# Key logits of the second batch in an agent attention followed by a two-layer network: whole-row products into one bank

## The chip, the core and the metric

The kernel runs on one core of a Trainium2 chip. The metric is the device time of one execution in microseconds (us). The core has a matrix engine (TensorE, PE in the profile, with its weight loads listed apart as PEld), a vector engine (VectorE, DVE), a scalar engine (ScalarE, ACT), GpSimd (POOL) and a queue engine (SP) that issues DMAs. TensorE multiplies a stationary operand, which it loads first, with a moving operand, and writes into PSUM, which has eight banks. VectorE and ScalarE read PSUM.

## The reference

Two batches of 12480 queries, keys and values of 128 channels, and 49 agents per batch. The agents attend to the keys, the queries attend to the agents, and the result goes through a two-layer network with a PReLU between its layers:

```python
a2k = sm(agents, k)          # softmax over the keys of scale * agents @ k.T
agent_v = a2k @ v            # 49 x 128 per batch
q2a = sm(q, agents)          # softmax over the agents
x = (q2a @ agent_v).reshape(24960, 128)
h = x @ w_in                 # 128 -> 2048
g = maximum(h, 0) + alpha * minimum(h, 0)
out = g @ w_out              # 2048 -> 128
```

Softmax subtracts the maximum and adds 1e-9 to the sum. Everything is float32 outside.

## The kernel before

A prologue of some 62 us treats the first batch's keys and values and prepares the weights. Then comes one main loop of 416 steps: 52 groups of 480 queries, 8 steps (`NM`) for a group, two of the 16 blocks of 128 hidden channels a step. A step has two parts, which the loop at the end of the kernel writes out by hand. `g1(s + 2)` (line 968) multiplies the folded first layer with the softmax weights of the queries, three products for each of two halves, into a PSUM tile `h`; ScalarE takes relu of it into `rh` (line 974), and VectorE the remainder into `rl` (line 975). `g2(s)` (line 990) multiplies `rh` and `rl` with the second layer, six products for each half, into a PSUM tile `acc`. All of these are half-array products: `TILES` names the rows 0 to 63 and 64 to 127, and each product runs over one half of the rows into a bank of its own, so that the two halves can run side by side. At the last step of each group, line 1001 adds three further half products, two on one half and one on the other; which half gets two alternates with the group.

Everything else is put between the steps by a table, `plan`, which says at which step which function is called: the queries' softmax for later groups (`q_...`), the outputs of earlier groups, and from step 16 on the second batch's keys, from step 96 on its values, and from 189 on the folding of its weights. There is no scheduler: each engine's order is the order in which the code issues.

The second batch's keys come in units of 512, which VectorE transposes into `kt` (line 538). `k_logits` is called for two units at a time, at steps 6, 9 and 14 of every 16 from step 16 on (`KEYS`), between the step's `g1` and its `g2`: twelve calls with two units of four blocks of 128 keys, and a thirteenth, at step 86, with the last unit, two blocks of 96 keys. For each block the keys are the stationary operand and the 49 agents the moving one. The products are plain float32, whereas the main loop's are in the one-pass form of float32. `pair_tile` gives a tile of two banks; the first half of the channels is multiplied into the first bank and the second half into the second. One step later, ahead of that step's `g1`, `k_take` has ScalarE copy the first bank's logits into `s` (line 572), and VectorE add the second bank's to them (line 574). `k_max_keys` on VectorE then takes a maximum of `s`.

Of the kernel before, what the change touches and what calls it, by code (L numbers as in the profile page):

```python
# [13 lines left out]
ALU = mybir.AluOpType  # L14
# [41 lines left out]
def kernel(  # L56
# [11 lines left out]
    nc = tc.nc  # L68
    B, N, C = q.shape
    NA = agents.shape[1]  # L70
# [9 lines left out]
    UB = KT // P  # L80
# [25 lines left out]
    TILES = ((0, HALF), (HALF, P))  # L106
# [3 lines left out]
    def pair_tile(name, i=None):  # L110

        i = (step[0] // NM + 1) % 2 if i is None else i
        return late[i].tile([P, 2, 512], F32, tag="x", name=name)


    def blocks(u):

        n = min(KT, N - u * KT)
        nb = -(-n // P)
        assert n % nb == 0  # L120
        return u * KT, n // nb, nb


    def wide(p):
# [25 lines left out]
    st = [  # L150
        dict(rows=2 * NA, cols=2 * C + 2) if b else {} for b in range(B)
    ]
# [215 lines left out]
    kv = {}  # L368
# [170 lines left out]
        kv["kt", b, u] = kt  # L539

    def k_logits(b, us):
        t = pair_tile(f"kl{b}_{us[0]}")
        tiles = [(t[:, i, :], r0, r1) for i, (r0, r1) in enumerate(TILES)]
        got = kv["kl", b, us[0]] = []
        c0 = 0
        for u in us:
            _, rows, nb = blocks(u)
            kt = kv.pop(("kt", b, u))
            for n in range(nb):
                c = c0 + n * NA  # L550
                for d, r0, r1 in tiles:
                    nc.tensor.matmul(  # L552
                        d[0:rows, c : c + NA], lhsT=kt[r0:r1, n * rows : (n + 1) * rows],
                        rhs=st[b]["ag"][r0:r1, 0:NA], start=True, stop=True,
                    )
            if got and got[-1][1] == rows:
                got[-1][2] += nb
            else:
                got.append([u, rows, nb, c0, [d for d, _, _ in tiles]])
            c0 += nb * NA  # L560

    def scores(b, u):
# [1 line left out]
        return st[b]["s"][0:rows, u * UB : u * UB + nb, :]  # L564

    def k_take(b, us):
        for u, rows, nb, c0, ds in kv.pop(("kl", b, us[0])):
            to = st[b]["s"][0:rows, u * UB : u * UB + nb, :]
            lg = [
                d[0:rows, c0 : c0 + nb * NA].rearrange("p (n a) -> p n a", a=NA) for d in ds  # L570
            ]
            nc.scalar.copy(out=to, in_=lg[0])
            for x in lg[1:]:
                nc.vector.tensor_tensor(out=to, in0=x, in1=to, op=ALU.add)

    def k_max(b):

# [469 lines left out]
    with tc.manual_schedule():  # L1047
# [18 lines left out]
        for p in range(NPK):  # L1066
            at(4 * p, k_turn, p)
            a, b = divmod(p, 2)
# [25 lines left out]
        for n in range(7):  # L1094
            load, ops = (load_win, narrow_win) if n < 4 else (load_wo, narrow_wo)
            s = SLABS[n]
# [11 lines left out]
        def more():  # L1108
            f = next(loads, None)
            if f is not None:  # L1110
                f[1](*f[2:])
            return f

        while n_in < N_IN:
            f = more()
            n_in += f[1] not in (q_load_rows, load_alpha, load_late)
        for s in range(max(plan) + 1):
            for f, a in plan.pop(s, ()):
                f(*a)
                if f.__name__ == "total" or f in (k_turn, k_mix):  # L1120
                    while True:
                        f = more()
# [40 lines left out]
        for g in range(NGT):  # L1163
            s0 = g * NM
            at((g + 1) * NM + OUT[0], o_take, g)
            d = OUT[1 if g % 2 == 0 or g == NGT - 1 else 2]
# [14 lines left out]
        for c, (lo, hi) in enumerate(pieces):  # L1181
            s0 = KEYS_FROM + c // len(KEYS) * 16
            turn, log, top = KEYS[c % len(KEYS)]
            us = tuple(range(lo, hi))
            for u, s in zip(us, turn):
                load(load_kb, "k", u, s0 + s)
                at(s0 + s, k_transpose_dve, 1, u)
            at(s0 + log, k_logits, 1, us)
            pre(s0 + log + 1, k_take, 1, us)
            if hi != NU - 1:  # L1190
                at(s0 + top, k_max_keys, 1, min(c, len(parts) - 1))
            last = s0 + top
        at(last + 1, k_max, 1)
        assert last + 3 < VALUES_FROM
        for c, (lo, hi) in enumerate(parts):
            s0 = VALUES_FROM + c // len(VALUES) * 16
            steps, av = VALUES[c % len(VALUES)]
            us = list(range(lo, hi))
# [57 lines left out]
```

## Time and profile before

| | |
|---|---|
| time, median of 3 runs | 987.12 us (987.0 to 988.08) |
| span of the profiled execution, first to last instruction | 985.9 us |
| the median lies above that span by | 1.2 us |
| TensorE, products | 971.7 us busy, 99% of the span |
| TensorE, weight loads | 927.0 us, 94% |
| VectorE | 837.7 us, 85% |
| ScalarE | 626.4 us, 64% |

The profile is of one execution. Its span runs from the first instruction to the last; the time of a run also has what lies around that. Loads and products of TensorE overlap, and products overlap each other, so their busy times do not add up to a length of work: what counts is the distance from one start to the next. A product in plain float32 leaves two records, each with a load of its own.

### The profile page before, as it was taken

Reading aid. Unit: us, or ns where it says so; the run is one execution under the profiler, and the core shown is the slowest. Engines: PE = TensorE matmul, PEld = TensorE weight load, DVE = VectorE, ACT = ScalarE, POOL = GpSimd, SP = SyncE. Lnnn points to the kernel's source line nnn. Section 1 sums busy time; section 2 is a strip of 40 time slices with the busy share of each in tenths; the row PEclk is TensorE's granted clock in tenths of the full one; section 3 lists DMA queues with packets and bytes.
Section 4 is the critical chain, followed back from the end, with each engine's and each line's share of the span. In section 5 each row is a group of like instructions: output and inputs, shape, how many; then the busy total and the mean of one; then the engine's idle time right before and its main releaser. Section 6 shows DMA issues by size and latency. Waiting matters only on the chain.

```text
span 985.9 us, 21716 instructions
## 1 busy us (share of the span) xinstructions
PE 971.7 (99%) x9046; PEld 927.0 (94%) x9046; DVE 837.7 (85%) x1054; ACT 626.4 (64%) x779; POOL 89.8 (9%) x67
## 2 busy tenths in 40 slices
PE   8989999999999999999999999999999999999997
PEld 5658999999989999999987999999999999999997
DVE  7887988998899999999987788788878887888775
ACT  5765655655667767777765666666666666666563
POOL 0011011011011011001101101100110111011100
PEclk9999999999999999999999999999999999999999
DMA  9933354444234234234312222212221223121201
GB/s 342 361 51 63 65 84 87 81 70 88 42 75 80 62 73 95 45 70 95 65 31 44 42 51 41 53 37 46 52 53 31 42 55 56 35 41 33 42 11 31
DMA packets 281027, 69.51 MB, mean 71 GB/s; under 512 B 259119, under 2 KB 273953, under 8 KB 280929
## 3 DMA queue, kind: packets, MB, share of 16 engines
q1 hardware_dynamic: 279937, 68.00, 33.0%
q8 instruction: 71, 1.16, 0.5%
q10 hardware_dynamic: 992, 0.12, 0.1%
q14 instruction: 27, 0.22, 0.1%
HBM read 42.59 MB, written 12.78 MB: 56 GB/s over the span
## 4 chain that ended last, share of the span: by engine, by line
PE 94%; DVE 2%; DMA 2%; ACT 1%; issue 0%; SPq 0%; ACTq 0%
PE acc L990 55%; PE h L968 27%; PE lg L864 2%; PE kl L552 2%; PE acc L1001 2%; PE av L650 1%; PE qsum L923 1%; DMA kw<-in_k_dram 1%; DMA win<-in_moe_w_in_dram 1%; PE a_ps L726 0%; DVE red L414 0%; PE avw L471 0%; PE ktp L388 0%; PE lin_ps L784 0%; PE etp L451 0%
## 5 line engine op out<-in xcount | busy, mean ns | idle before, releaser
L975 DVE SCALAR_TENSOR_TENSOR rl<-h,rh 128x960 fp32r<-128x960 f32 x416 | 478.2, 1150 | 123.1 <-ACT rh L974 120.8
L974 ACT ACTIVATE rh<-h 128x960 fp32r<-128x960 f32 x416 | 404.3, 972 | 270.1 <-PE h L968 262.1
L968 PE MATMUL h<-qmh,sab 64*128 64x480 f32 x1664 | 401.3, 378 | 0.7 <-DVE rl L975 0.5
L990 PE MATMUL acc<-rh,wl 64*128 64x480 f32 x1664 | 400.3, 378 | 0.0
L990 PE MATMUL acc<-rh,wh 64*128 64x480 f32 x1664 | 398.0, 375 | 0.0
L990 PE MATMUL acc<-rl,wh 64*128 64x480 f32 x1664 | 313.2, 377 | 0.0
L968 PEld LDWEIGHTS h<-qmh,sab 64*128 64x128 f32 x1664 | 247.2, 185 | 7.5 <-DVE rl L975 2.5
L990 PEld LDWEIGHTS acc<-rh,wl 64*128 64x128 f32 x1664 | 246.9, 184 | 5.9 <-issue 2.3
L990 PEld LDWEIGHTS acc<-rh,wh 64*128 64x128 f32 x1664 | 247.6, 184 | 2.9
L990 PEld LDWEIGHTS acc<-rl,wh 64*128 64x128 f32 x1664 | 223.6, 184 | 3.2
L968 PE MATMUL h<-qml,sab 64*128 64x480 f32 x832 | 222.7, 377 | 0.0
L894 POOL PARTITION_ALL_REDUCE qm<-qs x26 | 85.6, 3293 | 768.0 <-DVE qs L890 731.3
L968 PEld LDWEIGHTS h<-qml,sab 64*128 64x128 f32 x832 | 128.0, 185 | 1.7 <-DVE qml L912 0.2
L1006 ACT COPY os<-acc 128x480 f32<-128x480 f32 x52 | 29.2, 561 | 33.8 <-PE acc L1001 33.6
L1007 DVE TENSOR_TENSOR os<-acc,os 128x480 f32<-128x480 f32 x52 | 33.9, 651 | 2.7 <-ACT os L1006 2.4
L1012 DVE STREAM_TRANSPOSE ot<-os 128x480 f32<-128x480 f32 x52 | 34.7, 668 | 0.0
L903 ACT ACTIVATE qmh<-qs,padb 128x960 fp32r<-128x960 f32 x26 | 28.5, 1097 | 9.2 <-DVE qs L899 9.2
L1017 DVE TENSOR_TENSOR ot<-ot,qr 128x480 f32<-128x480 f32 x52 | 33.6, 645 | 0.1
L899 DVE TENSOR_TENSOR qs<-qs,qm 128x960 f32<-128x960 f32 x26 | 29.8, 1148 | 0.5 <-POOL qm L894 0.5
L890 DVE TENSOR_TENSOR qs<-qs,qw 128x960 f32<-128x960 f32 x25 | 28.7, 1148 | 1.7 <-DMA qw<-qs 1.7
L912 DVE TENSOR_TENSOR qml<-qs,qmh 128x960 fp32r<-128x960 f32 x26 | 29.8, 1148 | 0.0
L827 DVE STREAM_TRANSPOSE qt<-qin 128x960 f32<-128x960 f32 x25 | 29.2, 1167 | 0.0
(172 smaller groups left out, 802.8 us busy)
## 6 DMA issues: line engine op xcount, KB each, us to landing
out_dram<-ot SPq DMA_DIRECT2D x206, 60.0 KB
qin<-in_q_dram SPq DMA_DIRECT2D x200, 60.0 KB
qw<-qs SPq DMA_DIRECT2D x50, 240.0 KB
kw<-in_k_dram SPq DMA_DIRECT2D x12, 512.0 KB
vw<-in_v_dram SPq DMA_DIRECT2D x12, 512.0 KB
kb<-in_k_dram SPq DMA_DIRECT2D x96, 64.0 KB
v<-in_v_dram SPq DMA_DIRECT2D x24, 256.0 KB
win<-in_moe_w_in_dram SPq DMA_DIRECT2D x4, 512.0 KB
```

Source lines behind the costliest of these rows:

```text
L827: nc.vector.transpose(out=flat(t), in_=gq.pop(("in", k)).rearrange("p h t i -> p (h t i)"))
L894: nc.gpsimd.partition_all_reduce(flat(t), flat(gq["s", k]), P, ReduceOp.max)
L899: nc.vector.tensor_tensor(out=t, in0=t, in1=gq.pop(("m", k)), op=ALU.subtract)
L912: nc.vector.tensor_tensor(out=m, in0=gq["e", k], in1=gq["mh", k], op=ALU.subtract)
L968: nc.tensor.matmul(h[:, u, 0:GT], lhsT=w[a][r0:r1, f0 : f0 + P], rhs=x[r0:r1, :], start=n == 0, stop=n == 2,)
L974: nc.scalar.activation(out=rh, in_=h[:, :, 0:GT], func=AF.Relu)
L975: nc.vector.scalar_tensor_tensor(out=rl, in0=h[:, :, 0:GT], scalar=0.0, in1=rh, op0=ALU.max, op1=ALU.subtract)
L990: nc.tensor.matmul(acc[:, i, 0:GT], lhsT=a[r0:r1, 2 * m + u, :], rhs=x[r0:r1, u, :], start=m == 0 and n == 0, stop=False,)
L1006: nc.scalar.copy(out=t, in_=acc[:, 0, 0:GT])
L1007: nc.vector.tensor_tensor(out=t, in0=acc[:, 1, 0:GT], in1=t, op=ALU.add)
L1012: nc.vector.transpose(out=t.rearrange("p t i -> p (t i)"), in_=oo.pop(g))
L1017: nc.vector.tensor_tensor(out=t, in0=t, in1=gq.pop(("r", g)).to_broadcast([P, TB, 32]), op=ALU.mult)
```

## The change

`k_logits` multiplies each block of keys in one product over all 128 channels into the first bank of the pair tile, in place of two half products into two banks. `k_take` has ScalarE copy the finished logits; VectorE's additions are gone. The steps at which the functions are called are the same.

```diff
     def k_logits(b, us):
-        t = pair_tile(f"kl{b}_{us[0]}")
-        tiles = [(t[:, i, :], r0, r1) for i, (r0, r1) in enumerate(TILES)]
-        got = kv["kl", b, us[0]] = []
+        t = pair_tile(f"kl{b}_{us[0]}")[:, 0, :]
+        got = []
+        kv["kl", b, us[0]] = t, got
...
             for n in range(nb):
                 c = c0 + n * NA
-                for d, r0, r1 in tiles:
-                    nc.tensor.matmul(
-                        d[0:rows, c : c + NA], lhsT=kt[r0:r1, n * rows : (n + 1) * rows],
-                        rhs=st[b]["ag"][r0:r1, 0:NA], start=True, stop=True,
-                    )
+                nc.tensor.matmul(
+                    t[0:rows, c : c + NA], lhsT=kt[:, n * rows : (n + 1) * rows],
+                    rhs=st[b]["ag"][:, 0:NA], start=True, stop=True,
+                )
...
     def k_take(b, us):
-        for u, rows, nb, c0, ds in kv.pop(("kl", b, us[0])):
-            to = st[b]["s"][0:rows, u * UB : u * UB + nb, :]
-            lg = [
-                d[0:rows, c0 : c0 + nb * NA].rearrange("p (n a) -> p n a", a=NA) for d in ds
-            ]
-            nc.scalar.copy(out=to, in_=lg[0])
-            for x in lg[1:]:
-                nc.vector.tensor_tensor(out=to, in0=x, in1=to, op=ALU.add)
+        t, got = kv.pop(("kl", b, us[0]))
+        for u, rows, nb, c0 in got:
+            nc.scalar.copy(
+                out=st[b]["s"][0:rows, u * UB : u * UB + nb, :],
+                in_=t[0:rows, c0 : c0 + nb * NA].rearrange("p (n a) -> p n a", a=NA),
+            )
```

On TensorE, around the first call (step 22), the order before is this; `kl` is the logits' tile, `h` and `acc` those of `g1` and `g2`:

```order
L968 MATMUL h_1629<-qmh_1242,sab_858 128x480 x2
L552 MATMUL kl_0_1646<-ag_159,kt_0_1483 128x49 x8
L552 MATMUL kl_0_1646<-ag_159,kt_1_1457 128x49 x8
L990 MATMUL acc_1459<-rh_1576,wl 128x480 x2
L990 MATMUL acc_1459<-rh_1576,wh 128x480 x2
```

And now, with the line numbers of the changed kernel:

```order
L965 MATMUL h_1629<-qmh_1242,sab_858 128x480 x2
L551 MATMUL kl_0_1646<-ag_159,kt_0_1483 128x49 x4
L551 MATMUL kl_0_1646<-ag_159,kt_1_1457 128x49 x4
L987 MATMUL acc_1459<-rh_1576,wl 128x480 x2
L987 MATMUL acc_1459<-rh_1576,wh 128x480 x2
```

The place is the same; 16 half products have become 8 whole ones. On VectorE the order around the same call was:

```order
L538 STREAM_TRANSPOSE kt_2_1615<-kb_1024_1396 128x512
L975 SCALAR_TENSOR_TENSOR rl_1637<-h_1629,rh_1636 128x960
L574 TENSOR_TENSOR s_1214<-kl_0_1646,s_1214 128x392
L975 SCALAR_TENSOR_TENSOR rl_1690<-h_1682,rh_1689 128x960
L591 TENSOR_REDUCE mx_1215<-s_1214 128x49
```

and is now:

```order
L538 STREAM_TRANSPOSE kt_2_1615<-kb_1024_1396 128x512
L972 SCALAR_TENSOR_TENSOR rl_1637<-h_1629,rh_1636 128x960
L972 SCALAR_TENSOR_TENSOR rl_1681<-h_1673,rh_1680 128x960
L588 TENSOR_REDUCE mx_1215<-s_1214 128x49
L1004 TENSOR_TENSOR os_1709<-acc_1459,os_1709 128x480
```

The addition is gone, and nothing else has moved. ScalarE's, GpSimd's and the queue engine's orders are the same in both kernels.

## Rows read from the trace of the kernel before

**Rows 1.** The page: busy time of each engine (share, instructions), and the chain.

```profile
PE 971.7 (99%) x9046; PEld 927.0 (94%) x9046; DVE 837.7 (85%) x1054; ACT 626.4 (64%) x779; POOL 89.8 (9%) x67
...
PE 94%; DVE 2%; DMA 2%; ACT 1%; issue 0%; SPq 0%; ACTq 0%
```

**Rows 2.** Windows: stretch, its us, busy PE, PEld, DVE, ACT, POOL (instructions), clock, DMA.

```profile
117.00:277.00 160.00, 160.00 (x1666) 159.07 (x1664) 141.06 (x171) 94.17 (x109) 13.26 (x4) 1.00 0.43 76
```

**Rows 3.** Waits, 117 to 282 us: who waited for whom, total, times, longest.

```profile
DVE rl L975 <- ACT rh L974: 17.4, 33, 1.7
```

**Rows 4.** Tile kl: instructions, durations in ns (min/median/max), first and last start, forms.

```profile
L552 PEld LDWEIGHTS kl<-ag,kt x392: 158/188/189, 120.6 to 275.6; 64*128 64x128 f32 x192, 64*96 64x96 f32 x4
L552 PE MATMUL kl<-ag,kt x392: 201/272/273, 120.8 to 275.6; 64*128 64x49 f32 x192, 64*96 64x49 f32 x4
L572 ACT COPY s<-kl x13: 228/487/488, 122.8 to 276.5; 128x392 f32<-128x392 f32 x12, 96x98 f32<-96x98 f32 x1
L574 DVE TENSOR_TENSOR s<-kl,s x13: 247/546/567, 124.5 to 278.5; 128x392 f32<-128x392 f32 x12, 96x98 f32<-96x98 f32 x1
```

**Rows 5.** Timeline of PE, first burst: start us, us, what, form, count.

```profile
120.60 0.43 PE L968 MATMUL h<-qmh,sab 64*128 64x480 f32 x2
...
122.52 0.51 PE L990 MATMUL acc<-rh,wl 64*128 64x480 f32 x2
122.82 0.42 PE L990 MATMUL acc<-rh,wh 64*128 64x480 f32 x2
```

**Rows 6.** Timeline of PE around the last, short burst.

```profile
274.99 0.39 PE L968 MATMUL h<-qml,sab 64*128 64x480 f32 x2
275.21 0.39 PE L968 MATMUL h<-qmh,sab 64*128 64x480 f32 x2
...
276.01 0.38 PE L990 MATMUL acc<-rh,wh 64*128 64x480 f32 x2
```

**Rows 7.** Timeline of PE around line 784, 16 whole-array products.

```profile
75.27 0.37 PE L968 MATMUL h<-qmh,sab 64*128 64x480 f32 x2
...
79.67 0.38 PE L990 MATMUL acc<-rh,wh 64*128 64x480 f32 x2
```

**Rows 8.** Timeline of PE around line 738, one whole-array product.

```profile
85.76 0.38 PE L968 MATMUL h<-qml,sab 64*128 64x480 f32 x2
85.98 0.39 PE L968 MATMUL h<-qmh,sab 64*128 64x480 f32 x2
...
87.04 0.38 PE L990 MATMUL acc<-rh,wh 64*128 64x480 f32 x2
```

**Rows 9.** Timeline of PE around line 677, one product of 98 rows, two columns.

```profile
502.51 0.39 PE L968 MATMUL h<-qmh,sab 64*128 64x480 f32 x2
502.83 0.33 PE L677 MATMUL den<-x,pair 98*98 98x2 f32 x2
...
503.42 0.38 PE L990 MATMUL acc<-rh,wh 64*128 64x480 f32 x2
```

**Rows 10.** Timeline of the weight loads, line 509: two loads for a one-column product.

```profile
60.53 0.30 PEld L509 LDWEIGHTS den_ps<-den_sum,both 128*128 128x128 f32 x2 [0.17 <-issue]
```

**Rows 11.** Timeline of PE around line 702, two products, four records.

```profile
515.82 0.58 PE L968 MATMUL h<-qmh,sab 64*128 64x480 f32 x2
...
517.30 0.38 PE L990 MATMUL acc<-rh,wh 64*128 64x480 f32 x2
```

**Rows 12.** Timeline of PE around the three half products of line 1001.

```profile
507.78 0.38 PE L990 MATMUL acc<-rh,wh 64*128 64x480 f32 x2
...
508.65 0.38 PE L1001 MATMUL acc<-qml,zh 64*128 64x480 f32 x1
508.65 0.58 PE L968 MATMUL h<-qmh,sab 64*128 64x480 f32 x2
```

**Rows 13.** Lines 784 and 726: durations of products of 128 and of 512 columns, ns.

```profile
L784 PE MATMUL lin_ps<-wo,lin x32: 275/275/377, 75.6 to 79.1; 128*128 128x128 f32 x32
L726 PE MATMUL a_ps<-win,avt x16: 592/592/697, 61.9 to 535.3; 128*128 128x512 f32 x16
```

More of the change, by code (lines that the diff above doesn't have):

```diff
@@ L558, in k_logits @@
             else:
-                got.append([u, rows, nb, c0, [d for d, _, _ in tiles]])
+                got.append([u, rows, nb, c0])
             c0 += nb * NA
```

## The prediction

> **What bounds the kernel now.** I read the page first, for the engine that is never idle: TensorE's multiplications are busy for 971.7 of 985.9 us, and the chain that ended last is TensorE for 94% of its length [rows 1]. Then the stretch that the change touches: the 13 key-logit bursts (`k_logits`) run from 120.8 to 275.6 us [rows 4], and in 117 to 277 us TensorE is busy for 160.00 of 160.00 us, VectorE for 141.06 and ScalarE for 94.17 [rows 2]. In that stretch VectorE waits for ScalarE's `rh` for 17.4 us [rows 3], and no row of the waits has TensorE waiting for either. So here a microsecond more or less on TensorE is one on the end, and VectorE's work is covered as long as it is less than TensorE's. A busy TensorE need not be a fast one, so the third reading is the pitch: how long after one pair of half products the next one starts. It is 0.22 us in the main loop inside the stretch [rows 6] and outside it [rows 8], so nothing in the stretch is drawn out.
>
> **How a burst is priced.** I take the start of the last main-loop pair before a burst (line 968) and the start of the second main-loop pair behind it (line 990); the first behind it is skipped because its record contains its wait. Without a burst that distance would be two pitches, 0.44 us, in every case, so differences between cases need no further correction. A full burst takes 122.82 - 120.60 = 2.22 us [rows 5], thus 1.78 us of its own for 32 load-and-multiply records (each of its 16 half products in float32 leaves two). The two halves run side by side, so that is 16 turns of 0.111 us. The short last burst (96 keys instead of 128, two blocks) takes 276.01 - 275.21 = 0.80 us [rows 6].
>
> **Removed: half of TensorE's records.** 392 records become 196, all over 128 rows; the products have the same 49 columns. What paces a turn? Two whole-array loads of 128 columns, for products of a single column, take 0.30 us together where one load takes 0.188 [rows 10, 4]: they start 0.11 us apart, though there is next to nothing to multiply. So a load over 128 rows takes as long as two loads side by side over 64, and 16 turns stay 16 turns of about 0.11 us. I credit nothing for the halving.
>
> **Added: two changes of shape per burst.** The burst now stands, with the whole array, between half-array products. Four places of the trace of before do just that, in the main loop. The 16 float32 products of line 784 (32 records) take 79.67 - 75.27 = 4.40 us [rows 7]; the one product of line 738 (2 records) takes 87.04 - 85.98 = 1.06 us [rows 8]. The 30 records between them cost (4.40 - 1.06) / 30 = 0.111 us each, the same turn as in the bursts of today. What stays beside turns and the two pitches is 1.06 - 0.44 - 2 x 0.111 = 0.40 us: loads are no longer fetched ahead of the last products, and the other way round behind it. Today's bursts have nothing of this: 1.78 us is all turns. The last product's own length is in the 0.40: a product of 512 columns is 592 - 275 = 317 ns longer than one of 128 [rows 13], 0.83 ns a column, so 49 columns instead of 128 end 0.065 us sooner. A burst of 16 turns should thus take 1.06 + 14 x 0.111 - 0.065 = 2.55 us, which is +0.33. The other estimate starts at the narrowest such place, line 677, with loads of 98 columns and products of 2: 503.42 - 502.51 = 0.91 us for 2 records [rows 9]. By the 0.11 us of a load of 128 columns, one of 98 takes 0.083, 0.025 less; so 0.91 + 2 x 0.025 + 14 x 0.111 + 47 x 0.00083 = 2.55 us again. For the short burst: 0.91 + 2 further loads of 96 columns at 0.083 + 0.04 = 1.12 us against 0.80, +0.32. Together 12 x 0.33 + 0.32 = 4.3 us. I take that; bounds are 0.30 a burst, which is what line 677 leaves beside turns and pitches (0.91 - 0.44 - 2 x 0.083) with next to no product, and 0.40, if no product ends sooner: 3.9 to 5.2 us.
>
> **Added: the halves are brought into step.** At the end of each group of 8 steps line 1001 gives three half products to two halves. Starting in step, pairs then last 0.58 us instead of 0.38: one half lags by 0.20 [rows 12]. Today the next group's three products go the other way and close the gap again; the bursts in half rows leave it as it is. A whole-array burst must wait for the later half, and the earlier one loses its lead. Line 702 shows it: it begins with pairs of 0.58 us and takes 517.30 - 515.82 = 1.48 us for 4 records [rows 11], where 1.06 + 2 x 0.111 = 1.28 would be due: 0.20 more, measured from the half that leads. Averaged over the halves it is 0.10, and the average counts, because the three products would have cost the second half less the next time. The bursts stand at steps 6, 9 and 14 of 16, the three products at the ends of steps 7 and 15. So the bursts at 9 (four) and at 6 (five, of which the first starts at a lag of 0.05, pairs of 0.43 us in [rows 5]) lose 0.10, those at 14 nothing: 8 x 0.10 + 0.02 = 0.8 us. Bounds: nothing, if the main loop makes it up, and 1.0.
>
> **Removed: VectorE's additions.** Twelve of 0.546 us and one of 0.247 [rows 4], 6.8 us. They are covered wholly by TensorE today [rows 2, 3], so I count nothing for the end. ScalarE's copies stay, at their places. `k_max_keys` on VectorE now waits for the copy; the addition ahead of it waited for the same copy, so nothing new is held up behind it, and the `rl` of the step between them now goes first. The second bank is no longer used and the first is released earlier; no TensorE row waits for such a release, so that is zero too. If the cover were gone (a TensorE that is faster than VectorE there), the additions would be worth up to 6.8 us; with TensorE slower, as I expect, it grows.
>
> **The sum.** +4.3 + 0.8 = +5.1 us. All of it falls where TensorE is never idle, so nothing behind it absorbs it: later stretches shift as a whole. The profiled execution's span becomes 985.9 + 5.1 = 991.0 us. The median before, 987.12, lies 1.2 above that span, which does not change: 992.2 us.
>
> **Rivals.** *Loads pass one at a time (faster).* If the 32 records of today were a single row of loads, each 1.78 / 32 = 0.056 us, half as many would take 0.89 us. With the change of shape (0.335) that is 1.23 against 1.78, -0.56 a full burst, +0.14 for the short one, +0.8 for the lag: -5.7 us, 981.4. It decides from the point where a whole-array load takes under 0.09 us. The halving of the loads speaks for it; against it are the two loads 0.11 us apart [rows 10] and line 784's turns of 0.111. In the Trainium skill, page "TensorE: Matmul & The Clock Gate", Part 2, a load's time goes by its columns and not by its rows, which would make this rival's first half true; it does not say that loads of two halves queue, and the rows here have them side by side. Chance 0.04.
>
> *The change of shape is free here (same).* The waits at lines 784, 738, 677 and 702 could come from something else there, an operand that arrives late. Then 16 turns replace 16 turns, no lag is lost: 987.1. For it: the profile puts no name to most of these waits. Against: four places with different operands have the same cost within 0.05 us. Chance 0.04.
>
> *Loads and products take turns (much slower).* Side by side, a load may run under the other half's product; a whole-array load may have to wait until the product of the same rows is through. A turn is then 0.11 + 49 x 0.00083 = 0.15 us, a full burst 16 x 0.15 + 0.335 = 2.74 against 1.78, +0.95, the short one +0.5: 12 x 0.95 + 0.5 + 0.8 = +12.7 us, 999.8. Against it: line 784 has turns of 0.111 with loads of 0.11 and products of 128 columns that alone last 0.11, so there they do overlap [rows 7, 10, 13]. The Trainium skill, same page, Part 3 ("The mechanism"), says that a load overlaps running products only when their rows of the array differ, which is this rival; Part 2 of the page also allows it into a background buffer, which is what line 784 shows. Chance 0.06.
>
> **How the numbers follow.** The forecast, two shape changes a burst and the lag, has 0.86: 992.2 us. Its bounds are 3.9 and 6.2 us (5.2 + 1.0) above 987.12, 991.0 to 993.3; the runs before spread over 1.1 us, so I add 0.6 at the low and 0.5 at the high end: 990.4 to 993.8. The rivals lie outside and hold 0.14. What a measurement of this kernel can tell from no change is about 0.2%, 2 us: faster 0.04, same 0.04, slower 0.92.
>
> **What would show it.** In the profile after: 196 records at the logits' line over 128 rows, starting 0.11 us apart (0.056 for the first rival, 0.15 for the third); 2.5 to 2.6 us from the last pair before a full burst to the second behind it; pairs of 0.38 us behind each burst, and 0.58 ahead of those at steps 6 and 9; an idle stretch of the loads of about 0.3 us ahead of each burst; VectorE some 7 us less busy with no effect on the end. The forecast is wrong if the burst takes 2.2 us, or if the burst takes 2.55 and the span does not grow by it, because TensorE then had slack that I did not see.

## The result and the profile after

The changed kernel takes 993.26 us (median of 4 runs, 992.23 to 993.58) where the kernel before takes 987.60 (4 runs). The ratio is 1.0054 with a 95% interval of 1.0039 to 1.0068: slower by 3.9 to 6.7 us, where 5.1 were forecast. The profiled span is 991.8 us instead of 985.9.

The page of the changed kernel, busy times and chain (to be held against [rows 1]):

```profile
PE 979.2 (99%) x8850; PEld 912.9 (92%) x8850; DVE 832.4 (84%) x1041; ACT 626.5 (63%) x779; POOL 89.8 (9%) x67
...
PE 94%; DVE 4%; ACT 1%; issue 1%; ACTq 0%
```

TensorE has 196 records fewer (98 whole products stand in place of 196 half ones, two records each) and is busy for longer; the weight loads and VectorE are busy for less. The same stretch as in [rows 2], in the same columns, and the instructions of the logits' tile (the counterpart of [rows 4]), with what they waited for:

```profile
117.00:277.00 160.00, 160.00 (x1425) 141.32 (x1423) 132.27 (x155) 90.76 (x105) 13.26 (x4) 1.00 0.43 74
```

```profile
L551 PEld LDWEIGHTS kl<-ag,kt x196: 159/192/193, 121.7 to 281.3; 128*128 128x128 f32 x192, 128*96 128x96 f32 x4
L551 PE MATMUL kl<-ag,kt x196: 248/275/312, 121.7 to 281.3; 128*128 128x49 f32 x192, 128*96 128x49 f32 x4
L568 ACT COPY s<-kl x13: 232/487/488, 123.7 to 282.0; 128x392 f32<-128x392 f32 x12, 96x98 f32<-96x98 f32 x1
...
  issue: 4.4, 13
```

TensorE is as full as before, and in the same 160 us it gets through 1425 records instead of 1666. The halving of the logits' records accounts for most of the difference; the rest is work of the loop that now falls later. The additions' row is gone. A new one has come: the loads sat idle ahead of each of the 13 bursts, 4.4 us in all, 0.34 each. The timeline of the loads shows it at the first burst:

```profile
121.13 0.23 PEld L965 LDWEIGHTS h<-qmh,sab 64*128 64x128 f32 x2
121.69 1.86 PEld L551 LDWEIGHTS kl<-ag,kt 128*128 128x128 f32 x16 [0.34 <-issue]
123.61 0.19 PEld L987 LDWEIGHTS acc<-rh,wl 64*128 64x128 f32 x2
```

The products in the timeline of PE, first burst (step 22, see [rows 5]), second (step 25) and third (step 30):

```profile
121.35 0.42 PE L965 MATMUL h<-qmh,sab 64*128 64x480 f32 x2
121.69 1.99 PE L551 MATMUL kl<-ag,kt 128*128 128x49 f32 x16
123.61 0.48 PE L987 MATMUL acc<-rh,wl 64*128 64x480 f32 x2
123.93 0.38 PE L987 MATMUL acc<-rh,wh 64*128 64x480 f32 x2
...
127.19 0.37 PE L998 MATMUL acc<-qml,zh 64*128 64x480 f32 x1
127.20 0.59 PE L965 MATMUL h<-qmh,sab 64*128 64x480 f32 x2
...
129.59 0.59 PE L965 MATMUL h<-qmh,sab 64*128 64x480 f32 x2
130.11 1.99 PE L551 MATMUL kl<-ag,kt 128*128 128x49 f32 x16
...
132.35 0.37 PE L987 MATMUL acc<-rh,wh 64*128 64x480 f32 x2
...
141.69 0.38 PE L965 MATMUL h<-qmh,sab 64*128 64x480 f32 x2
142.01 1.99 PE L551 MATMUL kl<-ag,kt 128*128 128x49 f32 x16
...
144.25 0.38 PE L987 MATMUL acc<-rh,wh 64*128 64x480 f32 x2
```

From the last pair ahead to the second pair behind, the bursts take 2.58, 2.76 and 2.56 us, against 2.22 before. The later full bursts are alike: 2.59 to 2.62 us at step 6 of 16, 2.75 or 2.76 at step 9, 2.55 or 2.56 at step 14, and before the change 2.22 or 2.23 at every place. Behind line 998 (line 1001 before) the pairs last 0.59 us: the halves are 0.21 apart, and stay so until the second burst, behind which they last 0.37. The third burst starts with pairs of 0.38, and costs 0.20 less than the second.

The 0.34 us for which the loads sit idle is not itself the price. The first burst's products in the timeline of PE before the change, between the rows of [rows 5]:

```profile
120.81 1.93 PE L552 MATMUL kl<-ag,kt 64*128 64x49 f32 x32
```

They start 0.21 us behind the last pair (120.60); now it is 0.34 (121.69 after 121.35). So of the 0.36 us that the first burst takes longer, some 0.13 lie at its entry. With turns of the old length, the other 0.23 lie at its exit; this share is an estimate from the same rows.

The short last burst:

```profile
280.55 0.58 PE L965 MATMUL h<-qmh,sab 64*128 64x480 f32 x2
...
281.85 0.38 PE L987 MATMUL acc<-rh,wh 64*128 64x480 f32 x2
```

It takes 1.30 us, 0.20 of which is lag, against 0.80 in [rows 6].

How much of the 5.9 us of span lies in the changed stretch? Two marks that both kernels have are the products of the queries' sums (`qsum`) ahead of the first burst and behind the last. Before, then after, in the timelines of PE:

```profile
116.45 0.44 PE L923 MATMUL qsum<-qml,ones 64*128 64x480 f32 x2
...
305.15 0.38 PE L923 MATMUL qsum<-qml,ones 64*128 64x480 f32 x1
```

```profile
117.20 0.42 PE L920 MATMUL qsum<-qml,ones 64*128 64x480 f32 x2
...
311.03 0.38 PE L920 MATMUL qsum<-qml,ones 64*128 64x480 f32 x1
```

Between the marks are 188.70 us before and 193.83 after: +5.13 us. From the second mark to the end it is 680.8 us in both. The remaining 0.7 us lies ahead of the change: line 738's product, which no edit precedes, starts at 86.29 before and at 87.00 after, and in two of the kernels below, which have the same code up to there, at 85.01 and 87.04. So that part is a difference from run to run, and the distance between the marks is the better measure. I use it for the kernels below, one profiled execution of each; those for which no difference was expected agree to within 0.07 us.

| kernel | mark ahead | mark behind | between, us | to before |
|---|---|---|---|---|
| before | 116.45 | 305.15 | 188.70 | |
| after | 117.20 | 311.03 | 193.83 | +5.13 |
| half products, no addition | 116.94 | 305.64 | 188.70 | 0.00 |
| whole products, vector pass kept | 115.20 | 309.04 | 193.84 | +5.14 |
| whole products, two banks | 117.22 | 311.01 | 193.79 | +5.09 |
| products of one half only | 116.75 | 305.50 | 188.75 | +0.05 |
| half products, bursts cut | 116.69 | 305.46 | 188.77 | +0.07 |
| whole products, bursts cut | 116.11 | 313.83 | 197.72 | +9.02 |
| half products, fourth product | 116.95 | 306.63 | 189.68 | +0.98 |
| whole products, fourth product | 115.61 | 309.81 | 194.20 | +5.50 |

### The profile page after: what moved, and what is told of

Read it like the earlier page. It is cut to its first block, busy times and chain, and to the rows that moved or that the text cites. A ratio compares the mean times of both kernels' runs of the same rounds, so it can differ in the third digit from the quotient of the medians.

```text
span 991.8 us, 21311 instructions
## 1 busy us (share of the span) xinstructions
PE 979.2 (99%) x8850; PEld 912.9 (92%) x8850; DVE 832.4 (84%) x1041; ACT 626.5 (63%) x779; POOL 89.8 (9%) x67
## 4 chain that ended last, share of the span: by engine, by line
PE 94%; DVE 4%; ACT 1%; issue 1%; ACTq 0%
PE acc L987 55%; PE h L965 27%; PE kl L551 2%; PE lg L861 2%; PE acc L998 2%; PE av L647 1%; PE qsum L920 1%; DVE red L414 1%; PE a_ps L723 0%; PE ktp L388 0%; PE warm L203 0%; PE lin_ps L781 0%; DVE win L316 0%; ACT ktw L391 0%; PE avw L471 0%
## 5 line engine op out<-in xcount | busy, mean ns | idle before, releaser
L987 PEld LDWEIGHTS acc<-rh,wl 64*128 64x128 f32 x1664 | 242.4, 184 | 10.0 <-issue 2.3
L987 PEld LDWEIGHTS acc<-rh,wh 64*128 64x128 f32 x1664 | 242.9, 184 | 5.7
L987 PEld LDWEIGHTS acc<-rl,wh 64*128 64x128 f32 x1664 | 219.4, 184 | 7.0
```

The lines of the kernel that those rows point to most:

```text
L987: nc.tensor.matmul(acc[:, i, 0:GT], lhsT=a[r0:r1, 2 * m + u, :], rhs=x[r0:r1, u, :], start=m == 0 and n == 0, stop=False,)
```

## The experiments

**The additions alone.** The kernel before without line 574, so that the second half's logits are left out of the sum.

```diff
             nc.scalar.copy(out=to, in_=lg[0])
-            for x in lg[1:]:
-                nc.vector.tensor_tensor(out=to, in0=x, in1=to, op=ALU.add)
```

> The kernel before without the 13 additions on VectorE; the second half's logits are still multiplied but left out of the sum. My theory (VectorE's additions are wholly covered by TensorE): no difference to the kernel before, within 0.3 us in the span between the first and the last burst, a ratio of 1.000. Rival (VectorE holds TensorE back in this stretch): up to 6.8 us faster, the additions' own time.

Ratio 0.9999 (0.9990 to 1.0009), 0.00 us between the marks. VectorE's 6.8 us were covered entirely.

**The vector pass put back.** The changed kernel with a VectorE pass in the addition's place.

```diff
-            nc.scalar.copy(
-                out=st[b]["s"][0:rows, u * UB : u * UB + nb, :],
-                in_=t[0:rows, c0 : c0 + nb * NA].rearrange("p (n a) -> p n a", a=NA),
-            )
+            to = st[b]["s"][0:rows, u * UB : u * UB + nb, :]
+            lg = t[0:rows, c0 : c0 + nb * NA].rearrange("p (n a) -> p n a", a=NA)
+            nc.scalar.copy(out=to, in_=lg)
+            nc.vector.tensor_tensor(out=to, in0=lg, in1=to, op=ALU.max)
```

> The changed kernel with a VectorE pass of the same size put back where the addition stood (a maximum of the logits with themselves). My theory: the same time as the changed kernel, 5 to 6 us over the kernel before; a burst still takes 2.55 us from the last pair ahead of it to the second behind it. Rival (the missing addition is worth something and the change of shape costs more than read): more than 0.3 us slower than the changed kernel.

Ratio 1.0047 (1.0032 to 1.0062), 193.84 us between the marks, as in the changed kernel. The groups by line show that the pass was there:

```profile
L571 DVE TENSOR_TENSOR s<-kl,s 128x392 f32<-128x392 f32 (+1 forms) x13 | 6.8, 521 | 0.0
```

So 6.8 us of VectorE change nothing with either shape.

**Half of the products, no change of shape.** The kernel before with the products of the rows 0 to 63 alone, without additions.

```diff
-        tiles = [(t[:, i, :], r0, r1) for i, (r0, r1) in enumerate(TILES)]
+        tiles = [(t[:, i, :], r0, r1) for i, (r0, r1) in enumerate(TILES)][0:1]
...
-            for x in lg[1:]:
-                nc.vector.tensor_tensor(out=to, in0=x, in1=to, op=ALU.add)
```

> The kernel before with the second half's products and the additions left out: 16 records a burst instead of 32, all on the rows 0 to 63, no change of shape; the logits lack the second half of the channels. My theory (loads of the two halves pass side by side, a turn is one load of 0.11 us): a burst still holds up the loop by its 16 turns less what the other half runs ahead, at most one pitch of 0.22: 1.55 to 1.78 us of its own, at most 3 us faster in all. Rival (loads pass one at a time, 0.056 us each): 16 x 0.056 = 0.89 us a burst, 12 x 0.89 + 0.2 = 11 us faster than the kernel before.

Ratio 1.0001 (0.9992 to 1.0010), +0.05 us between the marks: no gain at all, where the rival had 11 us. The tile's instructions:

```profile
L552 PEld LDWEIGHTS kl<-ag,kt x196: 158/188/190, 121.0 to 275.9; 64*128 64x128 f32 x192, 64*96 64x96 f32 x4
```

With 196 loads instead of 392 the bursts hold the loop up for as long as before. The second half's loads had passed beside the first's.

**The banks.** The changed kernel with each unit's logits in a bank of its own.

```diff
-        t = pair_tile(f"kl{b}_{us[0]}")[:, 0, :]
+        pair = pair_tile(f"kl{b}_{us[0]}")
...
-        c0 = 0
-        for u in us:
+        for i, u in enumerate(us):
             _, rows, nb = blocks(u)
+            t, c0 = pair[:, i, :], 0
...
```

ScalarE's one copy (not shown) then reads both banks.

> The changed kernel with the second unit's logits in the second bank of the pair tile, in place of one bank for both; whole products, one copy by ScalarE. My theory: the number of banks plays no part, the same time as the changed kernel within 0.3 us in the stretch, each burst 2.55 to 2.65 us. Rival (writing all products of a burst into one bank is what slows it): back to 2.22 us a burst and to the kernel before.

Ratio 1.0056 (1.0041 to 1.0071), 193.79 us between the marks. The number of banks, which the change's name speaks of, has no part in it.

**More bursts, first attempt.** Each full burst cut in two, the first unit one step earlier, with half and with whole products. `k_logits` takes the unit to be multiplied as a further argument (not shown).

```diff
...
-            at(s0 + log, k_logits, 1, us)
+            if len(us) == 2:
+                at(s0 + log - 1, k_logits, 1, us, (0,))
+                at(s0 + log, k_logits, 1, us, (1,))
+            else:
+                at(s0 + log, k_logits, 1, us)
```

> The same cut made in the kernel before, where the products are half products: 12 more bursts, no change of shape. My theory: the same time as the kernel before, within 0.3 us in the stretch, since a burst of half products costs its turns alone. Rival (any interruption of the main loop costs something, whatever the shape): 12 x 0.33 = 4 us slower, as with whole products.

> The changed kernel with each of the twelve full bursts cut in two, four whole products one step earlier and four at the old place: twelve more entries and exits of the whole-array shape, the same products. My theory (each entry and exit costs 0.33 us together, whatever the number of products): 12 x 0.33 = 4.0 us slower than the changed kernel, about 9.5 us over the kernel before; each part takes 0.44 + 0.335 + 8 x 0.111 = 1.66 us from pair to second pair. Rival (the cost lies in the products themselves, a turn over 128 rows being longer): the same time as the changed kernel.

Ratios 1.0080 (1.0064 to 1.0097) and 1.0178 (1.0152 to 1.0203); neither theory was met, since the cut brought a wait of its own. The waits of PE in the half-product version, from 117 to 310 us, and a load row of the timeline:

```profile
PE kl L559 <- DVE os L1014: 4.8, 4, 1.2
```

```profile
208.81 0.97 PEld L559 LDWEIGHTS kl<-ag,kt 64*128 64x128 f32 x16 [1.61 <-DVE os L1014]
```

A part at step 8 takes the bank that was the accumulator of the group that has just ended, and waits for VectorE to read it, four times. The granted clock falls in both as well: to 0.91 in the mean of 200 to 220 us with half products, and to 0.89, 0.93 and 0.91 in three of the stretches of 20 us with whole ones. So the cut was made again at places clear of this wait.

**More bursts, clear of the wait.** The same cut, with the parts at steps 5 and 6, 9 and 10, 13 and 14.

```diff
-KEYS = (((1, 0), 6, 7), ((5, 3), 9, 14), ((9, 12), 14, 16))
+KEYS = (((1, 0), 6, 7), ((5, 3), 10, 14), ((9, 12), 14, 16))
...
```

> The cut of the bursts once more in the kernel before, but at steps 5 and 6, 9 and 10, 13 and 14, so that none of the parts falls on step 8, where the first cut had to wait for VectorE to read the bank. My theory: no difference to the kernel before, within 0.3 us between the queries' sums ahead of the first and behind the last burst (188.7 us); each part 0.89 us of its own. Rival (an interruption costs something in any shape): up to 4 us slower.

> The same cut in the changed kernel: the same whole products in 25 bursts instead of 13. My theory: 12 x 0.33 = 3.9 us slower than the changed kernel, 197.8 us between the same sums against 193.8, some 9.0 to 9.5 us over the kernel before (ratio 1.009). Rival (the cost lies in the products): as the changed kernel.

With half products: ratio 0.9999 (0.9990 to 1.0008), +0.07 us between the marks. With whole ones: ratio 1.0085 (1.0070 to 1.0100), 197.72 us between the marks, 3.89 more than the changed kernel, 0.32 for each of the 12 further bursts. One part in the timeline of PE, half products, then whole ones:

```profile
118.87 0.42 PE L975 MATMUL h<-qmh,sab 64*128 64x480 f32 x2
119.09 1.02 PE L559 MATMUL kl<-ag,kt 64*128 64x49 f32 x16
...
120.20 0.42 PE L997 MATMUL acc<-rh,wh 64*128 64x480 f32 x2
```

```profile
118.30 0.38 PE L970 MATMUL h<-qmh,sab 64*128 64x480 f32 x2
118.62 1.09 PE L556 MATMUL kl<-ag,kt 128*128 128x49 f32 x8
...
119.97 0.38 PE L992 MATMUL acc<-rh,wh 64*128 64x480 f32 x2
```

1.33 us against 1.67: 0.34 more for half as many records. Half products can be cut for nothing here. An entry and an exit of the whole-array shape cost the same together, whether 4 or 8 products stand between.

**The lag, first attempt.** The three bursts at steps 9, 11 and 14, in both kernels.

```diff
-KEYS = (((1, 0), 6, 7), ((5, 3), 9, 14), ((9, 12), 14, 16))
+KEYS = (((5, 3), 9, 10), ((8, 10), 11, 14), ((12, 13), 14, 16))
```

> The changed kernel with its three bursts of every 16 steps at steps 9, 11 and 14 in place of 6, 9 and 14, all in the odd group, so that two sets of the three half products of line 998, of opposite sense, lie between the burst at 14 and the next at 9. My theory of the lag (a lag opened by one set and ended by a burst costs about 0.1 us): the halves are nearly in step ahead of every burst, so each full burst takes 2.55 us and none 2.65; the stretch is 0.4 to 0.8 us shorter than in the changed kernel. Rival (the lag costs nothing on the whole, the main loop makes it up): the same time. VectorE's work is packed into fewer steps here; where TensorE waits for it, those waits are to be told apart in the trace.

> The same move in the kernel before. My theory: bursts of half products do not bring the halves into step, so their place is indifferent to a lag: the same time as the kernel before within 0.3 us in the stretch, but for waits for VectorE, whose work is packed closer. Rival (the place itself is better or worse): a difference like that of the changed kernel's move.

Ratios 1.0255 (1.0236 to 1.0275) and 1.0209 (1.0192 to 1.0226), some 25 and 20 us slower. Inconclusive for the lag: VectorE had not transposed the keys in time. The waits of PE, from 117 to 310 us, in the whole-product version:

```profile
PE kl L551 <- DVE kt L538: 7.2, 8, 1.3
```

These waits are 7.2 us of some 25. The granted clock falls as well, as the third figure from the end shows for the stretch from 260 to 280 us; how much of the rest is due to it was not worked out:

```profile
260.00:280.00 20.00, 18.74 (x138) 15.80 (x136) 12.54 (x18) 8.77 (x10) 0.56 (x1) 0.83 0.35 55
```

**The lag, without a move.** The fourth half product of line 1001, in both kernels, so that each half gets two.

```diff
-            jobs = ((0, "zh", mh), (1, "zl", mh), (1, "zh", ml))
-            if g % 2:
-                jobs = ((0, "zl", mh), (1, "zh", mh), (0, "zh", ml))
+            jobs = ((0, "zl", ml), (1, "zl", mh), (0, "zh", mh), (1, "zh", ml))
```

> The kernel before with a fourth half product at line 1001 (the product of the two low parts, which was left out before), two for each half, so that no lag arises. My theory: each of the 52 sets costs two pitches instead of one and a half, 0.109 us more: +5.7 us in all, +1.1 us between the two sums (ten sets). Rival (a lag is made up by the loop, an odd set costs two pitches as it is): no slower than the kernel before.

> The changed kernel with the same fourth half product. My theory: no lag ahead of any burst, each full burst 0.44 + 2.12 = 2.55 us and none 2.65; the whole products then cost only the changes of shape, +4.3 us over the kernel before with the same fourth product, against 5.1 without it. Rival (the lag has no part in it): again +5.1.

Ratios 1.0038 (1.0025 to 1.0051) and 1.0078 (1.0062 to 1.0095). With half products the fourth product costs 0.98 us between the marks (1.1 expected); over the whole run it is 2.5 to 5.0 us, less than the 5.7 that I had expected. So an odd set costs less than an even one, as the theory has it; why it is not half a pitch everywhere behind the second mark was not followed up. With it, whole products cost 194.20 - 189.68 = 4.52 us over half ones, against 5.13 without it. The second burst, which had the largest lag, in the timeline of PE:

```profile
128.18 0.40 PE L965 MATMUL h<-qmh,sab 64*128 64x480 f32 x2
128.52 1.99 PE L551 MATMUL kl<-ag,kt 128*128 128x49 f32 x16
...
130.76 0.38 PE L987 MATMUL acc<-rh,wh 64*128 64x480 f32 x2
```

2.58 us instead of 2.76, and all twelve full bursts take 2.57 or 2.58 us in this kernel. The lag's share is thus 5.13 - 4.52 = 0.6 us, as far as the fourth product changes nothing else between the two kernels.

## Why the prediction was right

*TensorE is the bound in the stretch, and VectorE is covered.* Right: 6.8 us taken from VectorE, or put back, move the marks by 0.01 us or less.

*A turn of a whole-array product is as long as one of two half products side by side.* Right: the 16 records of a burst stand 1.86 us from the first load's start to the last load's end, with 0.19 for one load, so 15 turns take 1.67, 0.111 each. The faster rival falls with the one-half kernel: with half of the loads and no change of shape, nothing was won (+0.05 us). The slow rival, turns of 0.15, falls with the same 0.111; so does the rule cited beside it from the Trainium skill, "TensorE: Matmul & The Clock Gate", Part 3, that loads run under products only in other rows of the array. Here loads over all rows start 0.111 us apart, which is what two such loads take with next to no product (0.11 in [rows 10]); so each runs under the product before it.

*The change of shape costs 0.33 us a burst, 4.3 in all.* Right in kind, a little small: 2.56 us for a burst without lag, 0.34 over 2.22, and 4.52 us for all 13 with the lag taken out, 0.2 more than the term said. That the cost goes with the entries and exits, and not with the number of products between them, is shown by the cut: +3.89 us for 12 more, +0.07 for the same cut with half products. The rival by which it is free here falls. What holds TensorE up there stays open: the rows put the loads' idle time down to "issue", which names no releaser. The prediction's reason, that loads are no longer fetched ahead at either end, fits the rows at the entry and was not tested by itself.

*The lag costs 0.8 us.* Right in kind, a little large: 0.6. I had put 0.10 on the bursts at step 6 as on those at step 9. Of the four bursts at step 6 that were to have the full lag, three have most of it gone: the pairs ahead of them last 0.42, 0.45 and 0.43 us, and only those ahead of the short last burst 0.58. Three steps ahead of those three bursts the leading half seems to wait until VectorE has released `h`, which has two buffers. That `rl`, in the timeline of DVE, and the pairs, in that of PE:

```profile
153.12 1.12 DVE L972 SCALAR_TENSOR_TENSOR rl<-h,rh 128x960 fp32r<-128x960 f32 x1
```

```profile
153.82 0.81 PE L987 MATMUL acc<-rl,wh 64*128 64x480 f32 x4
154.30 0.55 PE L965 MATMUL h<-qmh,sab 64*128 64x480 f32 x2
154.62 0.45 PE L965 MATMUL h<-qml,sab 64*128 64x480 f32 x2
```

The pass on VectorE ends at 154.24, the next pair starts at 154.30, and the pairs last 0.45 us from there on, where they had lasted 0.59. The same happens ahead of the next two such bursts: passes that end at 194.07 and 233.94, pairs that start at 194.13 and 234.00. Ahead of the last burst the pass in question ends at 272.42, the pair starts only at 273.79, and the lag stays. The profile names no wait there; that it is one is read from these times. Most of the lead was lost at that wait instead of at the burst, so some of the price was paid all the same. My wording, that the burst at step 6 loses it, was wrong for these three; that the lead is lost once it is opened and not closed was right. Why the lag comes to 0.6 us and not to 0.8 is not shown.

*The sum.* +5.1 forecast, +5.13 between the marks. That they agree so closely is luck: the two misses of 0.2 us happen to cancel. The median came out 1.1 us above the forecast of 992.2; 0.5 of that is in the kernel before, whose median was 987.60 this time instead of 987.12. The run-to-run spread ahead of the changed stretch (85.0 to 87.0 us for the same product in these profiles) is larger than either.

## What to carry to other kernels

Splitting a product into two half-array products that run side by side costs TensorE nothing where the weight load sets the pace, as here with 0.111 us a turn either way; joining them saves instructions and another engine's addition, and still no time on TensorE. In a loop of half-array products a lone whole-array product pays for the shape going in and coming out, some 0.33 us here, so joined products belong in as few bursts as possible, or not in such a loop at all. And before an engine's relief is credited, see whether the engine that bounds the stretch ever waits for it.

## What had not been expected of the hardware

That halves which have run out of step stay so until something makes them wait: a pair that lasts 0.59 us instead of 0.38 has lost nothing yet, but the next full-array product takes the lead away (2.76 us for the burst behind such pairs, 2.56 for one without).

One of the four waits at step 8 in the first cut with half products was followed by a lower clock. The windows of 208 to 209, 210 to 212 and 214 to 215 us there; the clock is the third figure from the end:

```profile
208.00:209.00 1.00, 0.19 (x4) 0.19 (x4) 1.00 (x3) 0.61 (x1) 0.00 (x0) 1.00 0.68 108
...
210.00:211.00 1.00, 1.00 (x8) 0.81 (x7) 0.00 (x0) 0.00 (x0) 0.00 (x0) 0.64 0.73 116
211.00:212.00 1.00, 1.00 (x8) 0.85 (x6) 0.00 (x0) 0.00 (x0) 0.00 (x0) 0.50 0.72 115
...
214.00:215.00 1.00, 1.00 (x14) 0.92 (x14) 0.74 (x1) 0.71 (x2) 0.00 (x0) 1.00 0.75 119
```

The loads had stood still for 1.61 us until 208.81. In the window from 210 the granted clock fell, from 211 it was 0.50 (1.2 GHz), and from 214 it was 1.00 (2.4 GHz) again. The wait of the same kind at 128 us left it at 1.00, and so did the other two. So a wait may be followed by a stretch at the lower clock and then cost more than itself; why it was this one is not shown.
